# A table of reciprocals stored in another order, its spread as one load a block, and the loads of the output stage in another order on one queue

## The chip, the cores and the metric

The kernel runs on one core of one Trainium2 chip. The metric is the time of one execution in microseconds (us), as a median of several runs. Five engines take part: TensorE (PE; PEld is its weight load), VectorE (DVE), ScalarE (ACT), GpSimd (POOL) and SyncE (SP). SP computes nothing; it issues DMAs, in the order in which they stand in the program, and stops at each until what that DMA needs has happened. ACT and POOL can issue DMAs too, between their other instructions. All queues share 16 DMA engines.

## The reference

Two branches on the same 2048 tokens of width 1024 are mixed by a gate: `out = g * a + (1 - g) * b`. Branch a is attention with 32 heads of width 32, and its output product:

```python
g = sigmoid((x * gate_w).sum(-1, keepdims=True))
qkv = (x @ wqkv).reshape(B, S, 3, H, Dh).transpose(2, 0, 3, 1, 4)
p = softmax(einsum("bhqd,bhkd->bhqk", q, k) * Dh ** -0.5)
o = einsum("bhqk,bhkd->bhqd", p, v)
a = o.transpose(0, 2, 1, 3).reshape(B, S, D) @ wo
```

Branch b looks up one of 64 rows of `u` and `v` for each token and each of 32 router heads (top 1 of 8 times top 1 of 8), and sums `gelu(x . u[e]) * v[e]`. Everything is float32.

## The kernel before, in words

The first 620 us or so make the router, the queries, keys and values; then comes the attention, and from about 1644 us the output product.

**Attention.** Heads are numbered `h = 4 * g + j`, with g the group of four (G = 8) and j in it. A head has NT = 16 steps of 128 keys; `at(step, f)` hangs a piece of work on a step `h * NT + kt`. In a step TensorE makes scores into a ring of 7 PSUM banks (`scores`, L1317), ACT takes their exponential into one of 8 tiles P (L1327), and TensorE multiplies P with V (`pv`, L1338). The sum of P over keys goes three ways: VectorE adds most tiles into `acc` (L1367), POOL adds a few of them into the tile `accd` with accumulating DMAs (L1360, `accd<-P` in the profile), and `merge` (L1370) joins the two. A P tile that such a DMA reads can be written again only when the DMA is done.

**The reciprocals.** `finish` stores a head's unnormalized output to DRAM (`OD`, profile `od<-osb`). `norm_sums` stores its row of sums (`SMD`, profile `smd<-ssb`). For each group of four heads `load_r` loads the sums back as 128 rows of 64 (`rr<-smd`), and `norm_r` takes their reciprocal, multiplies with the gate and stores the result to the table `RD` in DRAM (`rd<-rr`).

**Output.** The 2048 tokens go in 8 blocks of W = 256. For block n, `load_o` loads the heads' outputs of the 8 groups (8 DMAs of 128 KB, `V<-od`), and `load_rb` loads the reciprocals, each row of the table copied to 32 partitions (this is the spread; `rb<-rd` for block 0, `accd<-rd` for the others). `RD` is laid out as group, j, token, so a spread is four DMAs, one for each j, in pieces of 1 KB. The tiles are shared: heads' outputs use the two buffers named V, spreads use the two named accd, so a load waits for the last reader of the block two before. Blocks 0 and 1 use plain products (`wo_mm`): `split_hi`, `split_lo` and `split_o` scale the heads' outputs and cut them into a high and a low part, and `wo_mm` multiplies. Blocks 2 to 7 use a scheme with seven half-size products P1 to P7 (class `Halves`, L963), whose factors on the weight side include T1 to T4; `load_t(i)` brings those from DRAM (tables `t0h`, `t0l` to `t3h`, `t3l`, 1 MB each), the first three into tiles that blocks 0 and 1 have done with. `scale_o(n)` scales a block's heads' outputs on VectorE (L1576), and `unit(n)` makes a block's products and stores its output from the tiles `osb` and `post` (which lies in `rb0`). `plain_out(0)` and `plain_out(1)` store blocks 0 and 1 from `post` as well (L1584, L1586), so the second has to wait until the first's stores have read it.

The last group's reciprocals (kc = KC - 1 = 7) come last, as they need the last head's sums. The order written out by hand in L1597 to L1657 fits blocks 0 and 1, the last reciprocals and the loads of the T factors round that. Work of one engine runs in the order in which it is written.

Of the kernel before, what the change touches and what calls it, by code (L numbers as in the profile page):

```python
# [9 lines left out]
F32 = mybir.dt.float32  # L10
F32R = mybir.dt.float32r
# [5 lines left out]
S = 2048  # L17
D = 1024
H = 32
KC = D // 128  # L20
HC = KC // 2
NT = S // 128
NQ = S // 512
G = H // 4
W = 256
# [6 lines left out]
def gated_mha_peer_kernel(ctx, tc, xT, wqkv, wv, wo, wq, k12, ug, v, out):  # L32
# [8 lines left out]
    nc = tc.nc  # L41
# [4 lines left out]
    dram = ctx.enter_context(tc.tile_pool(name="dram", bufs=1, space=bass.MemoryType.DRAM))  # L46
# [7 lines left out]
    OD = [dram.tile([128, S], F32, name=f"od{g}") for g in range(G)]  # L54
    ZD = dram.tile([1, S], F32, name="zd")
    SMD = [dram.tile([4, S], F32, name=f"smd{g}") for g in range(G)]
    RD = dram.tile([G, 4, S], F32, name="rd")

    TD = [[dram.tile([128, KC // 2, 512], F32R, name=f"t{i}{part}") for part in "hl"] for i in range(4)]
    VPD = [dram.tile([128, D], F32R, name=f"vp{part}") for part in "hl"]  # L60
# [13 lines left out]
    def dma(dst, src, queue=nc.sync):  # L74
        a, b = (ap.bitcast(F32) if ap.dtype == F32R else ap for ap in (dst, src))
        return queue.dma_start(a, b)  # L76
# [16 lines left out]
    def split(hi, lo, src, on=None):  # L93
        nc.scalar.activation(hi, src, AF.Copy)  # L94
        (on or nc.vector).tensor_tensor(out=lo, in0=src, in1=hi.bitcast(F32), op=OP.subtract)
# [13 lines left out]
    def bank():  # L109
        i = bank_no[0] % 8  # L110
        bank_no[0] += 1
        return ps1.tile([128, 512], F32, name=f"bk{i}")
# [788 lines left out]
    zp = Pool("zp", side="right")  # L901
# [357 lines left out]
    wk = Pool("wk", bufs=2)  # L1259
# [88 lines left out]
    def rowsum(ps, *srcs):  # L1348
        for src in srcs:
            for qc in range(NQ):  # L1350
                yield nc.tensor.matmul(ps[32 * qc:32 * qc + 32, :], ones,  # L1351
                                       src[:, qc * 512:(qc + 1) * 512],
                                       start=(src is srcs[0]), stop=(src is srcs[-1]))
# [31 lines left out]
    def norm_sums(h, ps, queue=nc.sync):  # L1385
        g, j = divmod(h, 4)
        o = wk.tile([128, 512], F32, name="ssb")
        ins = nc.scalar.activation(o, ps, AF.Copy)
        dma(SMD[g][j:j + 1, :].rearrange("o (q s) -> (o q) s", q=NQ), o[::32, :], queue)
        return ins  # L1390


    def load_r(g):
        R[g] = wk.tile([128, 128], F32, name="rr", bufs=1)[:, :64]
        dma(R[g], SMD[g].rearrange("j (b m) -> (j b) m", m=64))

    def norm_r(g):
        r = R.pop(g)
        nc.vector.reciprocal(r, r)
        nc.vector.tensor_mul(r, r, G64)  # L1400
        dma(RD[g].rearrange("j (b m) -> (j b) m", m=64), r)


    OC, RB = {}, {}

    def load_o(n, k0, k1, queue=nc.sync):
        if k0 == 0:
            OC[n] = vpool.tile([128, KC, W], F32, name="V")
        for kc in range(k0, k1):
            dma(OC[n][:, kc, :], OD[kc][:, n * W:(n + 1) * W], queue)  # L1410

    def load_rb(n, k0, k1, js=range(4), queue=nc.sync):
        if k0 == 0 and js[0] == 0:
            RB[n] = rb0 if n == 0 else wk.tile([128, KC, W], F32, name="accd")
        for j in js:
            src = RD[k0:k1, j:j + 1, n * W:(n + 1) * W].rearrange("g j s -> j g s")
            dma(RB[n][32 * j:32 * j + 32, k0:k1, :], src.to_broadcast([32, k1 - k0, W]), queue)

    def load_chunk(n, k0, k1, queue=nc.sync):
        load_o(n, k0, k1, queue)  # L1420
        load_rb(n, k0, k1, queue=queue)
# [3 lines left out]
    OH, OL, W0 = {}, {}, []  # L1425
# [19 lines left out]
    def at(step, f, *a):  # L1445
        todo.setdefault(step, []).append((f, a))

    for h in range(H):
        base = h * NT
        g, j = divmod(h, 4)  # L1450
# [18 lines left out]
        at(28 * NT + 6 + i, dma, vhl[:, i], VPD[i])  # L1469
    at(29 * NT + 13, load_o, 0, 0, 4)  # L1470
    at(30 * NT + 7, load_o, 0, 4, KC - 1)
    at(30 * NT + 13, load_rb, 0, 0, KC - 1, range(2))
    at((H - 1) * NT + 2, load_rb, 0, 0, KC - 1, range(2, 4))
    at((H - 1) * NT + 8, load_rb, 1, 0, KC - 1)
    at((H - 1) * NT + 14, load_rb, 2, 0, KC - 1)


    BT = 2
# [34 lines left out]
    def load_at(n):  # L1513
        AT[n] = fin.tile([128, W], F32R, name="at", bufs=3)
        dma(AT[n], ATD[:, n * W:(n + 1) * W])
# [29 lines left out]
    def split_hi(kc):  # L1545
        nc.scalar.activation(woh[kc], raw_wo(kc), AF.Copy)
        if kc < KC - 1:
            o = OC[0][:, kc, :]
            nc.vector.tensor_mul(o, o, RB[0][:, kc, :])
            nc.scalar.activation(OH[0][:, kc, :], o, AF.Copy)  # L1550
# [10 lines left out]
    def load_t(i, *parts):  # L1561

        ops = ht.b.setdefault(f"T{i + 1}", [None, None])
        for n, (part, src) in enumerate(zip(parts, TD[i])):
            if part is None:
                continue
            m = HC // len(part)
            for j, place in enumerate(part):
                dma(place, src[:, m * j:m * j + m, :].rearrange("p k m -> p (k m)"))
            ops[n] = [place[:, k * 512:(k + 1) * 512] for place in part for k in range(m)]  # L1570
# [18 lines left out]
    def split_o(n, k0, k1):  # L1589
        o = OC[n][:, k0:k1, :]  # L1590
        nc.vector.tensor_mul(o, o, RB[n][:, k0:k1, :])
        split(OH[n][:, k0:k1, :], OL[n][:, k0:k1, :], o)

    def banks4():
        return {(i, half): bank() for i in range(W // 128) for half in range(2)}
# [4 lines left out]
    finish(H - 1)  # L1600
    sm = pso.tile([128, 512], F32, name="o")
    list(rowsum(sm, *(P[H - 1, NT - i] for i in (1, 2)), ACC.pop(H - 1)))
    load_o(1, 0, KC - 1, nc.gpsimd)
    split_hi(1)
    for kc in range(1, KC - 1):
        split_hi(kc + 1)
        if kc == 1:
            norm_sums(H - 1, sm, nc.scalar)
            load_r(G - 1)
            for n in range(2):  # L1610
                load_at(n)
            pso.close()
        split_lo(kc)
        wo_mm(pa, 0, [kc], False, False)
    norm_r(G - 1)
    for n in range(2):
        load_chunk(n, KC - 1, KC)
    load_rb(2, KC - 1, KC)
    split_lo(KC - 1)
    split(woh[0], wol[0], raw_wo(0))  # L1620

    load_t(2, None, [fin.tile([128, S], F32R, name="t3l")])
    load_t(0, *([keep.tile([128, S], F32R, name=f"wo_raw{j}")] for j in range(2)))
    ps_odd = Pool("ps_odd", space=PSUM)
    for (i, half), ps in pa.items():
        av_mm(0, i, half, ps)
    split_o(0, KC - 1, KC)
    wo_mm(pa, 0, [KC - 1], False, True)  # L1630
    OH[1] = zp.tile([128, KC, W], F32R, name="z1")
    OL[1] = wk.tile([128, KC, W], F32R, name="acc")
    for k0, k1 in ((0, HC), (HC, KC)):
        split_o(1, k0, k1)
    load_o(2, 0, KC)
    load_at(2)
    load_t(2, [zp.tile([128, S], F32R, name="z0")], None)
    load_t(1, *([keep.tile([128, S], F32R, name=f"wo_raw{2 + j}")] for j in range(2)))
    pa1 = banks4()
    wo_mm(pa1, 1, list(range(KC - 1)), True, False)  # L1640
    for (i, half), ps in pa1.items():
        av_mm(1, i, half, ps)
    plain_out(0, pa)
    load_t(3, *([part[k][:, 512:] for k in range(HC)] for part in (woh, wol)))
    load_rb(3, 0, KC, queue=nc.scalar)
    load_o(3, 0, KC)
    ht.places(wk.tile([128, S], F32R, name="acc"), "A11", "A12")
    ht.places(fin.tile([128, S], F32R, name="s31"), "S3", "S1")
    scale_o(2)
# [121 lines left out]
```

## Time and profile before

| | us |
|---|---|
| median of 3 runs | 1831.14 |
| lowest and highest | 1827.85, 1833.79 |
| the profiled execution, its own time | 1832.25 |
| span of that execution in the trace | 1830.4 |

| engine | busy us | share of the span |
|---|---|---|
| PE | 1817.8 | 99% |
| DVE | 1461.4 | 80% |
| ACT | 1312.5 | 72% |
| POOL | 231.7 | 13% |

The trace names a group of instructions by line, engine, operation and tiles (written from read), with buffer numbers left out. A time in square brackets is how long the engine stood idle before, with what ended that. In the chain of waits each line is a start, a length and what ran; it follows back from the last instruction to what released it. The DMA view can be cut to a stretch of time; for each queue (q1 is SP's, q10 ACT's, q0 POOL's) it then gives packets, MB, and the time of these packets as a share of 16 engines. PEclk and "granted clock" are the share of TensorE's full clock that it was given.

### The profile page before, as it was taken

To read this page: it belongs to the slowest core of one execution; us is meant where nothing else is said; L and a number is where in the kernel's file an instruction comes from. 1 tells how busy PE (TensorE), PEld (TensorE's weight loads), DVE (VectorE), ACT (ScalarE), POOL (GpSimd) and SP (SyncE) were. 2 spreads that over 40 slices of the span, in tenths; PEclk is the share of its full clock that TensorE was granted. 3 is DMA by queue.
4 is the path that set the end of the run, shared out by engine and by line. 5 is a ranking of instruction groups with operands and counts; after the bars stand their busy time and mean duration, and the time that the engine had idled before them with its cause. 6 is when DMAs were issued, how large, how long until landed. Compare 5 with 4: busy or idle time off the path is not lost.

```text
span 1830.4 us, 26559 instructions
## 1 busy us (share of the span) xinstructions
PE 1817.8 (99%) x10083; PEld 1099.8 (60%) x10083; DVE 1461.4 (80%) x1258; ACT 1312.5 (72%) x1716; POOL 231.7 (13%) x358
## 2 busy tenths in 40 slices
PE   9999999999999999999999999999999999999999
PEld 6777777788888644444444444444444444447787
DVE  7866876789967888888888888888888888884675
ACT  5545544522433699999999999999999999992221
POOL 1222222244001100000000000000000000010000
PEclk9999999999999999999999999999999999999999
DMA  7888689660267777776777777777777777776872
GB/s 271 277 277 280 209 296 286 199 215 9 83 240 247 219 157 178 158 177 154 177 176 164 186 165 182 171 173 167 174 186 159 178 159 182 174 138 180 281 164 78
DMA packets 127441, 345.24 MB, mean 189 GB/s; under 512 B 17168, under 2 KB 57904, under 8 KB 107920
## 3 DMA queue, kind: packets, MB, share of 16 engines
q1 hardware_dynamic: 95688, 193.40, 36.0%
q0 software_dynamic: 28224, 145.92, 34.1%
q10 hardware_dynamic: 3400, 4.20, 1.0%
q8 instruction: 80, 1.31, 0.3%
q14 instruction: 49, 0.40, 0.1%
HBM read 171.76 MB, written 72.36 MB: 133 GB/s over the span
## 4 chain that ended last, share of the span: by engine, by line
PE 88%; DMA 5%; issue 3%; DVE 1%; ACT 1%; SPq 1%; POOL 1%; DVEq 0%; ACTq 0%; POOLq 0%
PE ring L1317 28%; PE o L1338 25%; PE bk L302 15%; PE pa L963 5%; PE bk L724 5%; PE bk L982 2%; PE bk L290 2%; PE bk L341 2%; PE ring L1351 1%; PE bk L963 1%; SPq L76 1%; DMA accd<-rd 1%; DMA accd<-P 1%; DMA smd<-ssb 1%; DMA z<-t2h 1%
## 5 line engine op out<-in xcount | busy, mean ns | idle before, releaser
L1327 ACT ACTIVATE P<-ring 128x1024 f32<-128x1024 f32 (+2 forms) x1031 | 912.7, 983 | 14.5 <-DMA accd<-P 1.9
L1367 DVE TENSOR_TENSOR acc<-acc,P 128x2048 f32<-128x2048 f32 x319 | 730.9, 2291 | 72.6 <-ACT P L1327 47.1
L1338 PE MATMUL o<-P,V 128*32 128x512 f32 x3840 | 464.8, 599 | 0.0
L1317 PE MATMUL ring<-Q,K 98*128 98x512 f32 x1024 | 272.2, 407 | 0.4 <-ACT P L1327 0.3
L1317 PE MATMUL ring<-z,z 98*128 98x512 f32 x1020 | 270.6, 407 | 0.6 <-ACT accd L1327 0.6
L1317 PEld LDWEIGHTS ring<-Q,K 98*128 98x128 f32 x1024 | 182.0, 188 | 144.8 <-ACT P L1327 73.8
L1317 PEld LDWEIGHTS ring<-z,z 98*128 98x128 f32 x1020 | 181.3, 188 | 142.8 <-ACT P L1327 72.0
L1338 PEld LDWEIGHTS o<-P,V 128*32 128x32 f32 x3840 | 98.8, 109 | 223.1 <-issue 214.5
L1360 POOL DMA_DIRECT2D accd<-P x95 | 81.5, 858 | 931.5 <-ACT P L1327 406.5
L1365 DVE TENSOR_TENSOR acc<-P,P 128x2048 f32<-128x2048 f32 x32 | 73.4, 2293 | 74.8 <-ACT P L1327 74.8
L302 PE MATMUL bk<-xh,A 128*128 128x512 f32 x336 | 82.8, 396 | 0.0
L302 PE MATMUL bk<-xh,S 128*128 128x512 f32 x336 | 81.3, 393 | 0.0
L302 PE MATMUL bk<-xl,S 128*128 128x512 f32 x336 | 80.1, 391 | 0.0
L135 ACT ACTIVATE hi<-u 128x512 fp32r<-128x512 f32 x42 | 26.5, 632 | 70.0 <-issue 39.4
L302 PEld LDWEIGHTS bk<-xh,A 128*128 128x128 f32 x336 | 62.1, 188 | 23.8 <-issue 5.0
L1370 DVE TENSOR_TENSOR acc<-acc,accd 128x2048 f32<-128x2048 f32 x32 | 73.1, 2284 | 0.0
L302 PEld LDWEIGHTS bk<-xl,S 128*128 128x128 f32 x336 | 62.8, 188 | 16.3 <-issue 2.5
L302 PEld LDWEIGHTS bk<-xh,S 128*128 128x128 f32 x336 | 62.4, 188 | 14.5 <-issue 1.7
L1327 ACT ACTIVATE accd<-ring 128x1024 f32<-128x1024 f32 (+2 forms) x64 | 62.2, 1032 | 2.3 <-PE ring L1317 2.2
L963 PE MATMUL pa<-woh,acc 128*128 128x512 f32 x192 | 62.2, 389 | 0.0
L511 DVE TENSOR_TENSOR u<-u,bk 128x512 f32<-128x512 f32 x70 | 46.6, 682 | 10.0 <-DMA wpd<-u 5.8
L94 ACT ACTIVATE acc<-V 128x512 fp32r<-128x512 f32 x24 | 14.5, 625 | 50.8 <-DVE V L1576 14.4
(302 smaller groups left out, 2204.9 us busy)
## 6 DMA issues: line engine op xcount, KB each, us to landing
accd<-P POOLq DMA_DIRECT2D x95, 1024.0 KB, 7.6
wqt<-in_wq SPq DMA_DIRECT2D x64, 512.0 KB
wraw<-in_wqkv SPq DMA_DIRECT2D x28, 512.0 KB
kdh<-hi POOLq DMA_DIRECT2D x32, 256.0 KB, 5.3
kdl<-lo POOLq DMA_DIRECT2D x32, 256.0 KB, 6.5
qdh<-hi POOLq DMA_DIRECT2D x32, 256.0 KB, 5.9
qdl<-lo POOLq DMA_DIRECT2D x32, 256.0 KB, 5.9
z<-kdh SPq DMA_DIRECT2D x32, 256.0 KB
```

The costliest lines, as they stand in the source:

```text
L290: nc.tensor.matmul(b0[w, n], AW[PLAIN[w, ki]][a][:, k, :], X[f"B{ki + 1}{n + 1}"][b][:, k, :], start=first, stop=last)
L302: nc.tensor.matmul(ps, a[i][:, k, :], b[j][:, k, :], start=(k == 0 and i == j == 0), stop=(k == HC - 1 and i == 1))
L511: nc.vector.tensor_tensor(out=out, in0=a, in1=b, op=OP.add)
L724: nc.tensor.matmul(ps, x_part(a, t // 4, kc)[:, tok], b, start=first, stop=last)
L963: nc.tensor.matmul(ps, self.a[a][i][:, k, :], self.b[b][j][k], start=(not first and k == 0 and i == j == 0), stop=(k == HC - 1 and i == 1))
L1317: on_ring(nc.tensor.matmul(ring[:, i, :], K[:98, kt * 128:(kt + 1) * 128], Q[:98, qc * 512:(qc + 1) * 512], start=True, stop=True), i)
L1327: on_ring(nc.scalar.activation(P[h, kt][:, q0 * 512:(q0 + m) * 512].rearrange("p (a m) -> p a m", a=m), ring[:, i:i + m, :], AF.Exp, scale ...
L1338: nc.tensor.matmul(O[h][32 * qc:32 * qc + 32, :], Vt[g][:, kt, 32 * j:32 * j + 32], p[:, qc * 512:(qc + 1) * 512], start=(kt == 0), stop=( ...
L1360: nc.gpsimd.dma_start(ACCD[h], P[h, kt], accum_op=OP.add)
L1365: nc.vector.tensor_add(ACC[h], P[h, 0], P[h, kt])
L1367: nc.vector.tensor_add(ACC[h], ACC[h], P[h, kt])
L1370: nc.vector.tensor_add(ACC[h], ACC[h], ACCD[h])
```

## The change

1. `RD` is laid out as j, block, group, token within the block, so that a block's reciprocals of one j are 8 KB in one piece. `norm_r` stores into it with the indices to match.
2. `load_rb` is one DMA: 4 rows of up to 8 KB, each copied to 32 partitions. Before it was four DMAs.
3. In the attention loop block 0's spread was issued in two halves (head 30, step 13, and head 31, step 2); it is issued whole at the first place. Block 2's first seven groups were spread at head 31, step 14; that goes, and the whole spread of block 2 is loaded in the output stage.
4. Block 1's heads' outputs were loaded through POOL's queue right after the last head; they are loaded on SP behind the last sums. Block 3's spread was issued by ACT behind block 1's products; SP issues it, and block 3's heads' outputs, ahead of them.
5. `norm_r(G - 1)` stands inside the loop over kc, at kc = 4, instead of behind it. The first half of block 1 is scaled and split ahead of block 0's last group. Block 2's heads' outputs are loaded ahead of T1 instead of behind it.

```diff
-    RD = dram.tile([G, 4, S], F32, name="rd")
+    RD = dram.tile([4, S // W, KC, W], F32, name="rd")
...
-        dma(RD[g].rearrange("j (b m) -> (j b) m", m=64), r)
+        dma(RD[:, :, g, :].rearrange("j n (q m) -> (j n) q m", m=64), r)
...
-    def load_rb(n, k0, k1, js=range(4), queue=nc.sync):
-        if k0 == 0 and js[0] == 0:
+    def load_rb(n, k0, k1, queue=nc.sync):
+        if k0 == 0:
             RB[n] = rb0 if n == 0 else wk.tile([128, KC, W], F32, name="accd")
-        for j in js:
-            src = RD[k0:k1, j:j + 1, n * W:(n + 1) * W].rearrange("g j s -> j g s")
-            dma(RB[n][32 * j:32 * j + 32, k0:k1, :], src.to_broadcast([32, k1 - k0, W]), queue)
+        src = RD[:, n, k0:k1, :].rearrange("j g s -> j (g s)")[:, None]
+        dma(RB[n][:, k0:k1, :].rearrange("p g s -> p (g s)"),
+            src.to_broadcast([4, 32, (k1 - k0) * W]), queue)
...
-    at(30 * NT + 13, load_rb, 0, 0, KC - 1, range(2))
-    at((H - 1) * NT + 2, load_rb, 0, 0, KC - 1, range(2, 4))
+    at(30 * NT + 13, load_rb, 0, 0, KC - 1)
     at((H - 1) * NT + 8, load_rb, 1, 0, KC - 1)
-    at((H - 1) * NT + 14, load_rb, 2, 0, KC - 1)
...
-    load_o(1, 0, KC - 1, nc.gpsimd)
     split_hi(1)
     for kc in range(1, KC - 1):
...
             for n in range(2):
                 load_at(n)
+            load_o(1, 0, KC - 1)
             pso.close()
         split_lo(kc)
         wo_mm(pa, 0, [kc], False, False)
-    norm_r(G - 1)
+        if kc == HC:
+            norm_r(G - 1)
     for n in range(2):
         load_chunk(n, KC - 1, KC)
-    load_rb(2, KC - 1, KC)
+    load_rb(2, 0, KC)
     split_lo(KC - 1)
     split(woh[0], wol[0], raw_wo(0))
...
     load_t(2, None, [fin.tile([128, S], F32R, name="t3l")])
+    OH[1] = zp.tile([128, KC, W], F32R, name="z1")
+    OL[1] = wk.tile([128, KC, W], F32R, name="acc")
+    split_o(1, 0, HC)
+    split_o(0, KC - 1, KC)
+    load_o(2, 0, KC)
     load_t(0, *([keep.tile([128, S], F32R, name=f"wo_raw{j}")] for j in range(2)))
...
-    split_o(0, KC - 1, KC)
     wo_mm(pa, 0, [KC - 1], False, True)
-    OH[1] = zp.tile([128, KC, W], F32R, name="z1")
-    OL[1] = wk.tile([128, KC, W], F32R, name="acc")
-    for k0, k1 in ((0, HC), (HC, KC)):
-        split_o(1, k0, k1)
-    load_o(2, 0, KC)
+    split_o(1, HC, KC)
     load_at(2)
...
+    load_rb(3, 0, KC)
+    load_o(3, 0, KC)
     pa1 = banks4()
     wo_mm(pa1, 1, list(range(KC - 1)), True, False)
...
-    load_rb(3, 0, KC, queue=nc.scalar)
-    load_o(3, 0, KC)
```

## The prediction, made before the changed kernel was run

> **What bounds the kernel now.** I read the page first, then TensorE's waits, the chain of waits in order of time, the timelines round each gap, and the DMA view cut to short windows. The page says that TensorE is the bound:
>
> ```profile
> span 1830.4 us, 26559 instructions
> PE 1817.8 (99%) x10083; PEld 1099.8 (60%) x10083; DVE 1461.4 (80%) x1258; ACT 1312.5 (72%) x1716; POOL 231.7 (13%) x358
> ```
>
> So only about 12.6 us of the span are not matmul time, and part of that is the start and the end. The waits of TensorE from 1600 us on (waiting line, releaser, total, times, longest) are all that an edit of the last stages can win back directly:
>
> ```profile
> PE pa L963 <- DVE rb L969: 2.3, 1, 2.3
> PE pa L1522 <- ACT z L94: 1.4, 1, 1.4
> PE pa L963 <- ACT osb L1678: 0.8, 1, 0.8
> PE ring L1317 <- ACT P L1327: 0.3, 1, 0.3
> ```
>
> That is 4.5 us in the output stage and 0.3 us in the attention loop. The largest costs more than itself. In windows (stretch, length, busy time of PE, PEld, DVE, ACT, POOL, granted clock, DMA share, GB/s) the clock stays at 1.00 round the 1.4 us gap, and falls right after the 2.3 us one:
>
> ```profile
> 1660.00:1680.00 20.00, 18.61 (x82) 15.06 (x81) 9.82 (x12) 3.51 (x5) 0.00 (x0) 1.00 0.60 195
> 1722.00:1724.00 2.00, 1.27 (x3) 1.08 (x4) 1.97 (x4) 0.00 (x0) 0.00 (x0) 0.71 0.66 82
> 1724.00:1726.00 2.00, 2.00 (x6) 1.57 (x5) 1.22 (x3) 1.15 (x2) 0.00 (x0) 0.50 0.71 81
> 1726.00:1728.00 2.00, 2.00 (x9) 1.60 (x9) 2.00 (x4) 0.00 (x0) 0.00 (x0) 0.94 0.65 86
> ```
>
> 2 x (0.29 + 0.50 + 0.06) = 1.7 us are lost to the low clock. In all 4.5 + 1.7 = 6.2 us, 0.34%, is the most that the output stage can give.
>
> **What releases those gaps.** The chain (start, length, what):
>
> ```profile
> 1599.79 10.48 DMA accd<-P
> 1650.21 10.26 DMA smd<-ssb
> 1660.54 2.29 DMA rr<-smd
> 1663.70 1.46 DMA rd<-rr
> 1689.23 9.99 DMA z<-t2h
> 1740.03 13.60 PE pa L963 x60
> 1760.88 13.60 PE pa L963 x60
> ```
>
> The 1.4 us gap ends the serial path of the last head's sums: store, load, reciprocal, store to RD, spread, scale. Its first step is an 8 KB store that takes 10.26 us, because it stands behind other transfers. The last two rows are the same place in two later blocks, 20.85 us apart: a block's time without gaps. The 0.8 us gap waits for t2h. The 2.3 us gap waits for VectorE, which came late to a product's sums because block 3's heads (V<-od) came late.
>
> **The change, part by part.** *How wide the new spread is.* I read the number of engines off the small store of the sums, which has four rows. In the window 1632 to 1664 us it is all that the ScalarE queue carries (queue, packets, MB, share):
>
> ```profile
> q10 hardware_dynamic: 8, 0.01, 0.1%
> ```
>
> Eight packets are four rows and four completions, so four engines. The store od<-osb, whose DRAM side also begins with a dimension of 4, runs out between 1659.9 and 1661.4 us nearly alone:
>
> ```profile
> q1 hardware_dynamic: 23, 0.05, 7.7%
> ```
>
> 7.7% of 16 engines is 1.2 engines. The new load begins with 4 on the DRAM side (j, then 32 copies, then up to 8 KB), so I take four engines, with 32 pieces each; the old ones begin with 32. The other end, 16 engines, is a rival below. A piece of 8 KB, seen from 1676 to 1677.5 us where only such pieces run:
>
> ```profile
> q1 hardware_dynamic: 77, 0.63, 99.7%
> ```
>
> 1.5 x 16 x 0.997 / 77 = 0.311 us. A full block's spread is then 32 x 0.311 = 10.0 us on four engines, and one of 7 KB pieces 8.7 us. The old spread, in 1 KB pieces, from 1740 to 1746 us:
>
> ```profile
> q1 hardware_dynamic: 500, 0.48, 67.3%
> ```
>
> 0.48 MB in 6 us is 80 GB/s, 13 us for 1.05 MB, on all engines. So the load itself gets little shorter; twelve engines come free, and four carry all of it.
>
> *Block 0's spread, now in one piece (a loss).* Before, half of it went out at step 13 of head 30 and half at head 31. The issue on SP, ScalarE, the accumulating DMA behind it on POOL, and the waits:
>
> ```profile
> 1598.41 1.03 SPq L76 DMA_DIRECT2D rb<-rd  x2
> 1597.73 11.69 ACT L1327 ACTIVATE P<-ring 128x512 f32<-128x512 f32 x13
> 1599.79 0.86 POOL L1360 DMA_DIRECT2D accd<-P  x1 [13.26 <-ACT P L1327]
> 1610.35 3.77 ACT L1327 ACTIVATE P<-ring 128x512 f32<-128x512 f32 x4 [0.93 <-DMA accd<-P]
> 1611.00 0.50 PE L1317 MATMUL ring<-Q,K 98*128 98x512 f32 x1 [0.31 <-ACT P L1327]
> ```
>
> ScalarE already waits 0.93 us for this accumulation to release a P tile, and TensorE 0.31 us. Between 1599.6 and 1603 us the queues carry the first row, between 1605.2 and 1607.2 us the second:
>
> ```profile
> q1 hardware_dynamic: 313, 0.31, 54.3%
> q0 software_dynamic: 52, 0.43, 102.2%
> ```
>
> No accumulation packet (q0) ran while the spread (q1) did: on an engine the later transfer stands behind the earlier. Its eight pieces an engine take 8 x (2 x 16 x 1.022 / 52 = 0.63) = 5.0 us. The new spread holds four engines from about 1599.3 for 8.7 us, to 1608.0; the accumulation there ends at 1613.0 and lands at about 1613.3, not 1610.27. ScalarE then waits 3.05 us longer, and TensorE's eighth score matmul with it, as its ring bank is freed only then. ScalarE, which worked 11.69 us without a break ahead of that wait, can't win it back. The gap becomes 3.4 us, over the 2.3 us that dropped the clock, so up to 1.7 us more; as part of the slow window falls in the gap itself I take 1.3. Loss: 4.35 us. Bounds: 0 if the pieces interleave, 6.9 at the old 80 GB/s (0.92 MB in 11.5 us; 5.9 + 1.0).
>
> *Block 1's and 2's spreads, and the sums.* The rows that follow are VectorE in the loop over kc, TensorE at kc = 5 and at the gap, and a ScalarE pass:
>
> ```profile
> 1655.50 0.42 DVE L1556 TENSOR_TENSOR acc<-V,z 128x256 fp32r<-128x256 f32 x1
> 1656.17 1.22 DVE L1553 TENSOR_TENSOR wol<-wo_raw,woh 128x1024 fp32r<-128x1024 f32 x1
> 1661.38 1.07 PE L1522 MATMUL pa<-wol,z 128*128 128x512 f32 x4
> 1669.27 1.20 PE L1522 MATMUL pa<-woh,z 128*128 128x512 f32 x4 [1.39 <-ACT z L94]
> 1670.85 1.06 ACT L94 ACTIVATE z<-V 128x1024 fp32r<-128x1024 f32 x1 [1.63 <-DVE V L1591]
> ```
>
> Block 1's spread (head 31, step 8) has no accumulation behind it; issued near 1632, behind one accumulation, it ends by about 1646. Block 2's leaves the loop, and V<-od for block 1 leaves POOL's queue, so nothing stands ahead of the store of the sums at 1650.21. Like rd<-rr it then takes about 1.5 to 2.2 us, not 10.26. rr lands at about 1654.8. The reciprocal, now in the loop at kc = 4, comes to VectorE's turn at 1655.9: no wait. Its 0.8 us hides in the 4 us by which the splits lead TensorE (1657.4 against 1661.4); behind it are queued the splits of kc = 5 and 6, and were rr still as late as 1662.8, about 3 us of matmuls would wait for them. SP issues seven loads of block 1's heads (7 x 0.5, as in the row of 1598.41) ahead of rd<-rr, so that goes out at 1657.2 and is there at 1658.7; the spread of row 7 lands at about 1662. VectorE, 0.8 us later than before, does half of block 1 first (1.22, ScalarE 1.06, 1.22) and reaches block 0's last scale at 1666.1; its high half stands at 1667.1, ahead of the 1669.27 - 1.39 = 1667.9 at which TensorE needs it. Gain 1.4 us, with 0.8 to spare; each us that the sums come later than that brings back one of it.
>
> *The T loads and blocks 2 and 3.* SP issues block 2's spread at about 1660.7, four issues later, T3's low half, block 2's heads, T1, T3's high half, T2, block 3's spread, block 3's heads, then block 0's outputs. The program lets eight DMAs of SP and ScalarE be in flight, so an issue waits for the landing of the eighth before it; the old order paid for that here:
>
> ```profile
> 1672.59 15.92 SPq L76 DMA_DIRECT2D V<-od  x8
> SPq L76 <- DMA accd<-rd: 11.8, 4, 8.3
> ```
>
> In the new order the four engines carry the sum. With 2.5 us for each MB of T (421 GB/s, the 1676 window) and 2.7 for heads or outputs (1.54 MB in 4 us from 1708 on):
>
> ```profile
> q1 hardware_dynamic: 1069, 1.54, 103.6%
> ```
>
> Block 2's spread begins at 1663.4, after the two small ones. + 10.0 + 2.5 + 2.7 + 5.0 + 0.3 + 2.5 + 5.0 + 10.0 + 2.7 = 1704.1. T3 high lands by 1687, so the 0.8 us gap goes. Outputs of block 0 can't be issued before block 3's spread has landed (the eighth issue back from block 3's last head load), so the first lands at about 1705.8, where the old one let VectorE copy at 1704.88:
>
> ```profile
> 1704.88 0.69 DVE L1586 COPY rb<-pa 128x512 f32<-128x512 f32 x1 [3.16 <-PE pa L963]
> 1713.45 1.23 DVE L1576 TENSOR_TENSOR V<-V,accd 128x1024 f32<-128x1024 f32 x1 [3.99 <-DMA V<-od]
> 1721.90 1.41 DVE L969 TENSOR_TENSOR rb<-rb,pa 128x512 f32<-128x512 f32 x2
> 1722.73 0.67 PE L963 MATMUL pa<-z,s 128*128 128x512 f32 x1 [2.26 <-DVE rb L969]
> ```
>
> From the first copy to the sum that frees TensorE's bank it took 1722.6 - 1704.88 = 17.7 us, of which 3.99 + 0.61 were waits for V<-od. Without them 13.1 us: 1718.9, say 1719.2 as the outputs land one after another. So this matmul starts at 1719.2, not 1722.73: 3.5 us, in which the two small gaps are contained. TensorE would be ready at 1722.73 - 2.26 - 1.4 - 0.8 = 1718.3, so about 0.9 us of gaps stay, shorter than the 1.4 us one that left the clock alone: another 1.7 us. Gain 5.2 us. T4 lands by 1712 to 1713, about when its product starts. Later blocks ask 10.0 + 2.7 + 2.7 us of those four engines in 20.85 us, so the steady blocks stay covered.
>
> *Sum.* -5.2 + 4.35 = -0.85 us on the profiled 1832.25 (span 1830.4), which stands 1.1 us above the median. On the median, 1831.14 - 0.85 = **1830.3**.
>
> **The rivals.** *Interleaving (faster).* If an engine alternated between SP's and POOL's queues, the accumulation would need 8 x (0.63 + 0.27) = 7.2 us from about 1601.5 and land at 1609, before ScalarE asks. Then only the 5.2 us and the old 0.3 count: 1825.6. Against it stands the window without a q0 packet. [...]
>
> *All 16 engines (faster).* The new load doesn't narrow: 0.92 MB at 421 GB/s is 2.2 us, the accumulation isn't held, no gap of the output stage is left: 6.2 + 0.3, 1824.6. Against it: the od<-osb row. [...]
>
> *Reading one row 32 times stays slow (slower).* The four engines together get no more than the old 80 GB/s, 13 us a block. Block 0's spread then costs 6.9 us in the loop. Spreads 2 and 3 add 3 us each ahead of the outputs, so the bank comes free at 1725.2, 2.5 us later than before, and the low clock stays. Sum 9.4: 1840.5. It decides from about 11.7 us a block on: 3.4 us more ahead of the outputs eat the 3.5 gained there and keep the clock low, and the loop loses 4.35 + 1.5. For it: the only spreads seen run at this rate. Against it: they read one 1 KB row from 16 engines at once; now four engines read four rows.
>
> **How the numbers follow.** Chances: forecast 0.38, interleaving 0.13, 16 engines 0.14, slow rows 0.35. About 0.3%, 5.5 us, is what a measurement of this kernel can tell from no change. The forecast's own range is -4.5 to +4 (the clock kept or lost at either place, a spread 5% off), 1826.6 to 1835.1; three tenths of its chance lie past the bound, half on each side (0.06 and 0.06). The fast rivals lie at the bound or just past it: 0.23 of their 0.27 count as faster. Of the slow rows' 0.35, 0.31 count as slower. Faster 0.06 + 0.23 = 0.29; slower 0.06 + 0.31 = 0.37; the same 0.34. Range: from the fast rivals to the slow one, 1824 to 1841.
>
> **What would show it.** Right: a spread's packets number a quarter of the engines' share for 9 to 10 us; accd<-P near 1600 takes 13 to 14 us; ScalarE waits about 4 us there and TensorE over 3; smd<-ssb under 3 us; no wait of line 1522; the gap before the third block's second product under 2 us with the clock at 1.00. Wrong: accd<-P at 10 us or less, smd<-ssb still near 10, a spread over 12 us, or a wait for T or V that isn't named here.

## The result, and the profile after

The changed kernel takes 1853.31 us (median; 1851.34 to 1860.2) against 1830.97 us (1827.85 to 1833.97): ratio 1.0126, 95% interval 1.0106 to 1.0145. That is 22.3 us slower, and outside the predicted range of 1824 to 1841. The profiled execution took 1855.12 us.

The page of the changed kernel:

```profile
span 1853.3 us, 26507 instructions
PE 1820.4 (98%) x10083; PEld 1099.7 (59%) x10083; DVE 1461.5 (79%) x1258; ACT 1312.8 (71%) x1716; POOL 227.6 (12%) x351
```

The span grew by 22.9 us, TensorE's busy time only by 2.6. The other 20 us are idle time of TensorE. Its waits from 1590 us on, in the columns of the prediction:

```profile
PE pa L1527 <- DVE rb L1584: 15.5, 1, 15.5
PE ring L1317 <- ACT P L1327: 4.9, 1, 4.9
PE pa L963 <- DVE rb L969: 3.0, 1, 3.0
PE pa L963 <- DMA z<-t2h: 1.4, 1, 1.4
PE pa L963 <- DVE acc L95: 0.3, 1, 0.3
```

They sum to 25.1 us where before had 4.8. The old 1.4 us wait on the last sums is gone; the one in the attention grew from 0.3 to 4.9; and a new one of 15.5 us stands at the product (L1527) that needs a PSUM bank which `plain_out(1)` (VectorE's copy, L1584) has yet to empty. Windows round the two large ones (stretch, length, busy PE, PEld, DVE, ACT, POOL, granted clock, DMA share, GB/s):

```profile
1608.00:1614.00 6.00, 3.71 (x24) 1.62 (x23) 5.79 (x3) 2.43 (x3) 0.00 (x0) 0.94 0.25 71
1614.00:1620.00 6.00, 3.36 (x17) 0.89 (x17) 0.34 (x2) 3.77 (x4) 0.86 (x1) 0.50 0.57 137
1684.00:1690.00 6.00, 6.00 (x28) 4.99 (x27) 0.00 (x0) 0.00 (x0) 0.00 (x0) 1.00 0.25 87
1714.00:1722.00 8.00, 0.00 (x0) 0.00 (x0) 0.00 (x0) 0.00 (x0) 0.00 (x0) 0.82 0.25 79
1728.00:1732.00 4.00, 2.72 (x6) 2.15 (x7) 1.98 (x3) 1.51 (x3) 0.00 (x0) 0.50 0.92 300
```

Two things are to be seen. The clock is at half behind both gaps, which accounts for most of TensorE's 2.6 extra busy us. And the DMA share is 0.25 in the third and the fourth row: four engines of sixteen, for many us on end, at 79 to 87 GB/s, while every computing engine but TensorE is idle in the third and all of them in the fourth. The DMA view of the third stretch (queue, packets, MB, share of 16 engines):

```profile
q1 hardware_dynamic: 67, 0.52, 25.0%
```

6 x 4 / 67 = 0.36 us for a piece of 8 KB. SyncE's issues show who waits for the four engines (SPq rows are issues, x their number; the second of the two `accd<-rd` at 1668.32 is block 2's spread, issued at 1669.05):

```profile
1658.99 0.32 SPq L76 DMA_DIRECT2D rr<-smd  x1
...
1668.32 1.25 SPq L76 DMA_DIRECT2D accd<-rd  x2
1669.66 0.42 SPq L76 DMA_DIRECT2D t3l<-t2l  x1
1673.93 19.58 SPq L76 DMA_DIRECT2D V<-od  x8
1693.55 0.43 SPq L76 DMA_DIRECT2D wo_raw<-t0h  x1
...
1696.70 0.53 SPq L76 DMA_DIRECT2D accd<-rd  x1
1697.33 28.21 SPq L76 DMA_DIRECT2D V<-od  x8
1725.65 2.07 SPq L76 DMA_DIRECT2D out<-rb  x4
```

In these rows an issue waits for the landing of the eighth before it. So the seventh of block 2's heads waited until block 2's spread had landed, at 1690.9, and the eighth until T3's low half had, at 1693.2; T1's halves, T3's high half and all behind them went out from 1693.55 on. Block 3's heads were held in the same way by block 3's spread, and block 0's outputs, which stand behind them, went out at 1725.65. SP's own waits between 1660 and 1760 us say it in one row:

```profile
SPq L76 <- DMA accd<-rd: 28.8, 2, 14.6
```

These are two waits of about 14.5 us for a spread. In the attention, ScalarE waits for the accumulation, which now shares engines with block 0's spread:

```profile
1615.99 3.77 ACT L1327 ACTIVATE P<-ring 128x512 f32<-128x512 f32 x4 [5.56 <-DMA accd<-P]
```

### The profile page after: what moved, and what is told of

It is laid out like the page before. It is cut to its first block, busy times and chain, and to the rows that moved or that the text cites. A ratio compares the mean times of both kernels' runs of the same rounds, so it can differ in the third digit from the quotient of the medians.

```text
span 1853.3 us, 26507 instructions
## 1 busy us (share of the span) xinstructions
PE 1820.4 (98%) x10083; PEld 1099.7 (59%) x10083; DVE 1461.5 (79%) x1258; ACT 1312.8 (71%) x1716; POOL 227.6 (12%) x351
## 4 chain that ended last, share of the span: by engine, by line
PE 86%; DMA 8%; issue 3%; DVE 2%; ACT 1%; POOL 1%; SPq 1%; ACTq 0%; DVEq 0%; POOLq 0%
PE ring L1317 27%; PE o L1338 25%; PE bk L302 15%; PE bk L724 5%; PE pa L963 4%; DMA accd<-rd 3%; PE bk L982 2%; PE bk L290 2%; PE bk L341 2%; DMA accd<-P 2%; PE ring L1351 1%; DMA t3l<-t2l 1%; PE bk L963 1%; SPq L76 1%; DMA xl<-in_wo 0%
## 5 line engine op out<-in xcount | busy, mean ns | idle before, releaser
L1317 PE MATMUL ring<-Q,K 98*128 98x512 f32 x1024 | 272.2, 407 | 5.0 <-ACT P L1327 4.9
L1317 PE MATMUL ring<-z,z 98*128 98x512 f32 x1020 | 270.7, 407 | 0.8 <-ACT accd L1327 0.6
L1317 PEld LDWEIGHTS ring<-Q,K 98*128 98x128 f32 x1024 | 182.2, 188 | 149.3 <-ACT P L1327 78.4
L1317 PEld LDWEIGHTS ring<-z,z 98*128 98x128 f32 x1020 | 181.3, 188 | 143.1 <-ACT P L1327 72.3
L302 PEld LDWEIGHTS bk<-xh,S 128*128 128x128 f32 x336 | 62.4, 188 | 14.5 <-issue 1.7
```

Of the source, the lines that this page charges most:

```text
L302: nc.tensor.matmul(ps, a[i][:, k, :], b[j][:, k, :], start=(k == 0 and i == j == 0), stop=(k == HC - 1 and i == 1))
L1317: on_ring(nc.tensor.matmul(ring[:, i, :], K[:98, kt * 128:(kt + 1) * 128], Q[:98, qc * 512:(qc + 1) * 512], start=True, stop=True), i)
```

## The experiments

Three theories stood at the start. A: the one load is narrow, and four engines are what it costs. B: reading the same row of the table over and over is slow on any number of engines. C: the order on SP costs the time whatever form the spread has. In the table a ratio compares a kernel with runs of the kernel before from the same batch; those had medians from 1829.79 to 1831.93 us, so medians of different rows can't be told apart to less than 2 us.

| kernel | median us | ratio to before | 95% interval |
|---|---|---|---|
| changed kernel | 1853.31 | 1.0126 | 1.0106 to 1.0145 |
| new order, four loads of 8 KB pieces | 1824.92 | 0.9967 | 0.9957 to 0.9977 |
| old order, one load | 1855.62 | 1.0134 | 1.0112 to 1.0156 |
| new order, old layout, four loads of 1 KB pieces | 1845.15 | 1.0074 | 1.0055 to 1.0092 |
| old order, four loads of 8 KB pieces | 1825.78 | 0.9976 | 0.9967 to 0.9985 |
| changed, block 0's spread in two parts | 1860.62 | 1.0166 | 1.0145 to 1.0187 |
| changed, block 0's spread as four loads | 1850.62 | 1.0107 | 1.0090 to 1.0123 |
| changed, block 3's loads behind block 0's outputs | 1854.63 | 1.0136 | 1.0119 to 1.0152 |
| four loads, block 0's in the attention as one | 1832.65 | 1.0000 | 0.9991 to 1.0010 |
| four loads, blocks 2 and 3 as one | 1843.75 | 1.0065 | 1.0046 to 1.0084 |
| four loads, blocks 4 to 7 as one | 1829.47 | 0.9991 | 0.9979 to 1.0003 |

**Four loads of 8 KB pieces, new order.**

```diff
-        src = RD[:, n, k0:k1, :].rearrange("j g s -> j (g s)")[:, None]
-        dma(RB[n][:, k0:k1, :].rearrange("p g s -> p (g s)"),
-            src.to_broadcast([4, 32, (k1 - k0) * W]), queue)
+        for j in range(4):
+            src = RD[j:j + 1, n, k0:k1, :].rearrange("j g s -> j (g s)")
+            dma(RB[n][32 * j:32 * j + 32, k0:k1, :].rearrange("p g s -> p (g s)"),
+                src.to_broadcast([32, (k1 - k0) * W]), queue)
```

> The changed kernel, but a spread is four loads, one for each j, of 32 pieces of 8 KB (the table's new layout stays, the order stays). Theory A, the width: in the changed kernel a piece of 8 KB takes about 0.4 us of one engine, and 32 such pieces in a row on each of only four engines make the 13 to 15 us of a block; a load that starts with 32 runs on 16 engines, so a spread takes 3 to 4 us, accd<-P near 1600 about 11 us, the waits of 4.9 and 15.5 us go: about 1826 us. Theory B, the row: reading one row of the table again and again gives some 80 GB/s whoever reads it (1 KB pieces on all engines before, 8 KB pieces on four engines after); the spread then still takes 11 to 13 us, now on all engines, and the time stays at 1848 to 1858 us. Theory C, the order on SP: the outputs of block 0 still stand behind three spreads and the T loads; with short spreads that is about 6 us less than before, so about 1840 us.

Measured: 1824.92 us, ratio 0.9967. It is faster than before, as theory A said; B and C asked for 1840 or more. The page of this kernel:

```profile
span 1823.5 us, 26540 instructions
PE 1816.1 (100%) x10083; PEld 1098.1 (60%) x10083; DVE 1461.5 (80%) x1258; ACT 1312.4 (72%) x1716; POOL 227.5 (12%) x351
```

No wait of TensorE is left from 1590 us on, and the clock stays at 1.00; the window in which the changed kernel has its longest gap:

```profile
1690.00:1720.00 30.00, 30.00 (x134) 24.86 (x133) 14.48 (x22) 6.42 (x11) 0.00 (x0) 1.00 0.96 276
```

**The one load alone.** The old order and queues of the output stage; layout, `norm_r` and `load_rb` of the changed kernel. The expectation speaks of block 0's spread cut at group 4; the kernel that ran issues it whole at head 30, step 13, as the changed kernel does:

```diff
-    at(30 * NT + 13, load_rb, 0, 0, KC - 1, range(2))
-    at((H - 1) * NT + 2, load_rb, 0, 0, KC - 1, range(2, 4))
+    at(30 * NT + 13, load_rb, 0, 0, KC - 1)
```

> The kernel before with the new layout and the one-load spread alone; its order and queues stay. Block 0's spread is cut into groups 0 to 3 and 4 to 6, at the two steps where its halves stood. Theory A: every spread takes 13 to 15 us on four engines as in the changed kernel; block 2's seven groups issued at the end of head 31 hold the small store of the sums on those engines, so the sums come some us later than before, and block 3's spread lands late too: 1834 to 1842 us. Theory B: a spread costs what it did, 13 us: 1830 to 1834 us. Theory C, nearly all in the order: 1831 us, the same as before.

Measured: 1855.62 us. All theories had it too low, A by 14 us (and A for a spread of block 0 in two parts). The one load does the whole damage without the new order of the output stage; only the places differ:

```profile
PE ring L1317 <- ACT P L1327: 5.2, 1, 5.2
PE pa L1521 <- ACT z L94: 5.2, 1, 5.2
PE pa L963 <- ACT acc L94: 3.7, 1, 3.7
PE pa L963 <- DVE rb L969: 2.3, 2, 2.1
```

They sum to less than in the changed kernel, but TensorE is busy for 1826.8 us, 9.0 more than before, at a mean granted clock of 0.993 against 0.999.

**The order alone.** The changed kernel with the old `RD`, the old store and the old four loads in `load_rb`:

```diff
-        src = RD[:, n, k0:k1, :].rearrange("j g s -> j (g s)")[:, None]
...
+        for j in range(4):
+            src = RD[k0:k1, j:j + 1, n * W:(n + 1) * W].rearrange("g j s -> j g s")
+            dma(RB[n][32 * j:32 * j + 32, k0:k1, :], src.to_broadcast([32, k1 - k0, W]), queue)
```

> The changed kernel with the table's old layout and the old spread, four loads in pieces of 1 KB; the new order and the whole spread of block 0 at head 30, step 13, stay. Theory A: the old spread is on all engines and lets others in between its four parts; the wait for block 0's outputs falls from 15.5 to about 6 us, the head's wait stays near 5: about 1842 us. Theory B and theory C alike: a spread still takes 13 us, all engines are held meanwhile, and the outputs of block 0 stand behind two of them: 1848 to 1856 us. It parts A from the others: under 1845 for A, over 1848 for C.

Measured: 1845.15 us, between the two bounds. Two waits are left, the same two places as in the changed kernel:

```profile
PE pa L1527 <- DVE rb L1584: 9.7, 1, 9.7
PE ring L1317 <- ACT P L1327: 5.4, 1, 5.4
```

So the new order by itself, block 0's whole spread in the attention included, costs some 14 us with the old spread in 1 KB pieces. Theory C holds under a condition: the order is only as good as its spreads are short.

**Four loads of 8 KB pieces, old order.** The edit of the first experiment, made to the kernel before with the new layout; block 0's halves by j as before.

```diff
-    RD = dram.tile([G, 4, S], F32, name="rd")
+    RD = dram.tile([4, S // W, KC, W], F32, name="rd")
...
-            src = RD[k0:k1, j:j + 1, n * W:(n + 1) * W].rearrange("g j s -> j g s")
-            dma(RB[n][32 * j:32 * j + 32, k0:k1, :], src.to_broadcast([32, k1 - k0, W]), queue)
+            src = RD[j:j + 1, n, k0:k1, :].rearrange("j g s -> j (g s)")
+            dma(RB[n][32 * j:32 * j + 32, k0:k1, :].rearrange("p g s -> p (g s)"),
+                src.to_broadcast([32, (k1 - k0) * W]), queue)
```

> The kernel before with the new layout and a spread as four loads of 8 KB pieces (7 KB for seven groups), one for each j, that start with 32; its order, its queues and the two halves of block 0's spread stay as they were. With the new order the same four loads gave 1824.9 us. Theory A, the width and the pieces do it all: spreads of 6 us let the sums, t2h and block 3's heads arrive in time in the old order too: 1824 to 1826 us, no gap over 0.3 us. Theory C, the order does part of it: the small store of the sums still stands behind block 1's heads on GpSimd's queue and block 2's spread, and block 3's heads still come late: gaps of 1.4 and about 1 us stay, 1827 to 1831 us.

Measured: 1825.78 us, as theory A said; no wait of TensorE from 1590 us on. With four loads of 8 KB pieces the order makes no difference that can be told (0.9976 and 0.9967, intervals overlapping). With the two runs before this one the table has both orders for each of three forms of the spread: 1830.97 and 1845.15 (1 KB pieces), 1855.62 and 1853.31 (one load), 1825.78 and 1824.92 (four loads of 8 KB pieces). Block 0's spread goes out whole in the new order and in two halves in the old, but for the one load, where it is whole in both.

**The spreads by themselves.** Behind the last output of the kernel with four loads, twice:

```diff
+    X = wk.tile([128, KC, W], F32, name="accd")
+    for n in range(2):
+        for j in range(4):
+            src = RD[j, :, n, :]
+            dma(X[32 * j:32 * j + 32], src[None].to_broadcast([32, KC, W]))
+        src = RD[:, n].rearrange("j g s -> j (g s)")[:, None]
+        dma(X.rearrange("p g s -> p (g s)"), src.to_broadcast([4, 32, KC * W]))
+        for j in range(4):
+            src = RD[j:j + 1, n].rearrange("j g s -> j (g s)")
+            dma(X[32 * j:32 * j + 32].rearrange("p g s -> p (g s)"), src.to_broadcast([32, KC * W]))
+        for rows in (16, 128):
+            src = TD[n][0].rearrange("p k m -> p (k m)")[:rows][:, None]
+            dma(X.rearrange("p g s -> p (g s)"), src.to_broadcast([rows, 128 // rows, KC * W]))
```

> The changed kernel with four-load spreads, and behind its last output, twice over, loads of 1 MB each into one tile, so that one starts when the one before has landed: four loads of 1 KB pieces (eight rows of 1 KB for each j, each read 32 times), the one load of 4 rows of 8 KB, the four loads of one row of 8 KB each, one load of 16 rows of 8 KB with 8 copies of each, and one of 128 rows, each read once. They measure the spread with nothing beside it. Theory A, the width: 13 us, 32 x 0.31 = 10 us, 3 to 4 us, 3 us, 2.5 us. Theory B, the row: time goes with how often a row is read and how many engines read it at once: 13 us, 12 to 14 us, 6 us as seen inside the kernel, 2.5 to 4 us for 16 rows, 2.5 us. It tells whether the 13 to 15 us of a block in the changed kernel are its own or come from what runs beside it. The added loads lengthen the kernel by about their sum, some 70 us.

The run took 1922.48 us. Measured, in windows cut to the packets of each load (the first round's 1 KB form overlapped the last outputs and is left out): first round one load, four loads, 16 rows, 128 rows; second round 1 KB pieces and the same four.

```profile
1838.50:1850.90 12.40, 0.00 (x0) 0.00 (x0) 0.00 (x0) 0.00 (x0) 0.00 (x0) 0.50 0.23 85
1852.30:1857.30 5.00, 0.00 (x0) 0.00 (x0) 0.00 (x0) 0.00 (x0) 0.00 (x0) 0.50 0.91 210
1859.40:1864.40 5.00, 0.00 (x0) 0.00 (x0) 0.00 (x0) 0.00 (x0) 0.00 (x0) 0.50 0.92 210
1866.00:1869.60 3.60, 0.00 (x0) 0.00 (x0) 0.00 (x0) 0.00 (x0) 0.00 (x0) 0.50 0.80 291
1870.80:1883.50 12.70, 0.00 (x0) 0.00 (x0) 0.00 (x0) 0.00 (x0) 0.00 (x0) 0.50 0.44 83
1885.20:1900.60 15.40, 0.00 (x0) 0.00 (x0) 0.00 (x0) 0.00 (x0) 0.00 (x0) 0.50 0.23 68
1902.00:1907.30 5.30, 0.00 (x0) 0.00 (x0) 0.00 (x0) 0.00 (x0) 0.00 (x0) 0.50 0.91 198
1909.40:1914.10 4.70, 0.00 (x0) 0.00 (x0) 0.00 (x0) 0.00 (x0) 0.00 (x0) 0.50 0.91 223
1915.70:1919.20 3.50, 0.00 (x0) 0.00 (x0) 0.00 (x0) 0.00 (x0) 0.00 (x0) 0.50 0.85 300
```

With nothing beside it the one load takes 12.4 and 15.4 us at a share of 0.23, as long as the old form in 1 KB pieces (12.7). Four loads take 5.0 and 5.3. Both theories have a part: the width is worth a factor of 2.5 to 3, and reading rows again one of 1.3 to 1.5 (16 rows and four loads against 128 rows). The 10 us that A and the prediction expected were measured in neither round, and why the second took 3 us longer than the first isn't known.

**Which spreads cost.** The kernel with four loads, with the one load for some blocks only; the condition is `n == 0 and k0 == 0`, `n in (2, 3)` or `n >= 4`.

```diff
+        if n in (2, 3):
+            src = RD[:, n, k0:k1, :].rearrange("j g s -> j (g s)")[:, None]
+            dma(RB[n][:, k0:k1, :].rearrange("p g s -> p (g s)"),
+                src.to_broadcast([4, 32, (k1 - k0) * W]), queue)
+            return
```

> The changed kernel with four-load spreads everywhere (1824.9 us, no gap) except block 0's in the attention, which is the one load. It prices the stall in the attention against a clean output stage. From the changed kernel's trace: accd<-P 15 us, ScalarE's wait 5 to 6 us, TensorE's 4.4 to 5.2 us, and half a clock for 6.8 us, of which some 1.5 us are lost outside the gap. If nothing of it is given back: 1830 to 1832 us. Rival: the output stage has slack to give back, 1825 to 1828 us.

> The same with the one load for blocks 2 and 3 alone, four loads for all others. It prices the two spreads ahead of block 0's outputs. If they make the wait of 15.5 us: block 0's outputs go out 15 to 20 us later than in the kernel with four loads everywhere (1699.2), TensorE waits 10 to 16 us there, and the time is 1838 to 1845 us. Rival, that the spreads of blocks 4 to 7 keep the bound (each holds four engines for 12 to 15 us of a block's 20.85 us, beside heads and outputs): under 1835 us.

> The same with the one load for blocks 4 to 7 alone, four loads for all others. By themselves such loads took 12.25 and 15.25 us against 20.85 us for a block, so they should stay covered: 1825 to 1826 us, no wait. Rival: with the heads and the outputs on the same four engines they don't fit, and a wait of VectorE for the spread shows at each block, of some 2 us each: 1829 to 1834 us.

Measured: 1832.65, 1843.75 and 1829.47 us. By the ratios, against 0.9967 for four loads everywhere: 0.0033 x 1831 = 6.0 us for block 0, 17.9 for blocks 2 and 3, 4.4 for blocks 4 to 7. They sum to 28.3; the one load everywhere costs (1.0126 - 0.9967) x 1831 = 29.1. By the intervals each price is good to 2.5 to 4 us. Each has its own wait of TensorE. Block 0 as one load:

```profile
PE ring L1317 <- ACT P L1327: 5.0, 1, 5.0
```

Blocks 2 and 3 as one load (L1590 is the copy in `plain_out` again, six lines further down in this kernel):

```profile
PE pa L1533 <- DVE rb L1590: 14.8, 1, 14.8
```

Blocks 4 to 7 as one load:

```profile
PE pa L963 <- DVE rb L969: 3.3, 1, 3.3
```

The first run came out just above what was expected, 1832: nothing of the attention's stall is given back. The second came out as expected (block 0's outputs go out at 1718.25, 19 us later than with four loads everywhere): the two spreads ahead of block 0's outputs make the wait of 15.5 us. In the third I had expected no wait. Block 4's spread, issued behind the T4 loads, block 1's outputs and its own heads, lands 19.19 us later, and VectorE waits for it; a row of the chain and one of VectorE's timeline:

```profile
1713.82 19.19 DMA accd<-rd
```

```profile
1733.04 2.36 DVE L1580 TENSOR_TENSOR V<-V,accd 128x1024 f32<-128x1024 f32 x2 [10.26 <-DMA accd<-rd]
```

The rival had the right time, but not for its reason, a wait at each block: VectorE waits 10.26 us for block 4's spread and under 2 us for two later ones, and TensorE has one wait that counts, in block 3, while VectorE is late with scaling block 4.

**Block 3's loads later.**

```diff
-    load_rb(3, 0, KC)
-    load_o(3, 0, KC)
     pa1 = banks4()
...
     plain_out(0, pa)
+    load_rb(3, 0, KC)
+    load_o(3, 0, KC)
```

> The changed kernel with block 3's spread and heads' outputs issued by SP right behind block 0's outputs instead of ahead of block 1's products. The reading is that SP could issue block 0's outputs only at 1725.65 because block 3's spread had to land first, and that plain_out(1) and with it TensorE waited 15.5 us for them. If so, the outputs go out near 1704, the wait of 15.5 us falls under 3 us; block 3's heads come some 5 us later and the wait behind them (3.0 us) grows to 5 to 8 us: 1840 to 1847 us. Rival: the T loads set it, which are late in either order, and the heads of block 3 give it all back: 1850 us or more.

Measured: 1854.63 us, the rival's time. Block 0's outputs go out at 1697.43, and the wait of 15.5 us is gone, but others take its place. The two largest, and a row of the chain:

```profile
PE pa L963 <- ACT acc L94: 9.2, 1, 9.2
PE pa L963 <- DMA wol<-t3l: 3.9, 1, 3.9
```

```profile
1703.40 25.74 DMA accd<-rd
```

What holds block 3's heads is again block 3's spread, which lands 25.74 us after its issue, where by itself it took 12.4 and 15.4. SP issues it behind the T loads (from 1694.29 on) and block 0's outputs. So the T loads, the rival's cause, look to be a part of it. Four engines have the same work whatever the order; the order chooses who waits for them.

**Block 0's spread in two parts.**

```diff
-    at(30 * NT + 13, load_rb, 0, 0, KC - 1)
+    at(30 * NT + 13, load_rb, 0, 0, 4)
+    at((H - 1) * NT + 2, load_rb, 0, 4, KC - 1)
```

> The changed kernel, but block 0's spread goes out in two parts, groups 0 to 3 at head 30, step 13, and groups 4 to 6 at head 31, step 2 (the two places of before), each still on four engines. The reading of the two traces is that the whole spread holds the accumulation accd<-P (15.1 us) and costs 4.6 us of TensorE's wait and about 1.7 us of clock there. If that holds: accd<-P near 11 us, TensorE's wait under 1 us, and the time falls by 5 to 6.5 us, to about 1847 us, as all that follows comes that much earlier. Rival: the later part goes out near the load of block 1's spread and moves the stall on, or the last chain of loads doesn't start earlier: under 2 us of gain.

Measured: 1860.62 us, a miss of 13 us. The wait at L1317 fell only from 4.9 to 3.4 (accd<-P from 15.1 to 13.25): even four groups of seven keep the four engines busy beside the accumulation (issued at 1601.24; from 1608 to 1614 us the two queues take 19.0% and 4.7% of 16 engines, 3.8 engines). Waits sum to 22.7, less than in the changed kernel, but TensorE is busy for 1826.0 us, 5.6 more, as the clock is at half in three stretches of the output stage, where the changed kernel has one; one of them:

```profile
1723.00:1737.00 14.00, 4.91 (x12) 3.85 (x13) 3.89 (x6) 2.35 (x4) 0.00 (x0) 0.51 0.65 210
```

Why the output stage then waits where it does isn't settled by this run.

**Block 0's spread as four loads.** The changed kernel, with the four loads for `n == 0 and k0 == 0` alone.

> The changed kernel with block 0's spread alone as four loads (16 engines), all other spreads as one load. It prices the stall in the attention by itself: accd<-P near 1600 at 10 to 11 us, TensorE's wait there under 0.5 us and no drop of the clock. Theory A: the rest follows 6 us earlier, 1846 to 1848 us. Rival, after the run in which block 0's spread went out in two parts: what the attention wins, the output stage gives back in waits: 1851 to 1856 us.

Measured: 1850.62 us. The stall in the attention is gone, and SP's issue of block 0's outputs comes 7.6 us earlier (1718.02). The time falls by about 3 us, with overlapping intervals, not by the 6 that the same edit is worth in the other direction when the output stage is clean: the waits of 15.6 and 3.3 stay, and the mean granted clock is 0.994, as in the changed kernel, although that one has 6.83 us at half clock from the attention's stall.

## Why the prediction was wrong

*What held.* The bound: 6.2 us in the output stage and 0.3 in the attention were called the most that could be won there, and the kernel with four loads has no gap left at 1824.9 us, against the 1824.6 worked out for a load on all 16 engines. The width: four engines, from the store with four rows, is a share of 0.25 in the rows above. The stall in the attention: block 0's spread does hold up the accumulation, and ScalarE and TensorE wait for it; the size was 4.9 us of TensorE's wait, not 3.4, and 6.0 us of the time in the run that prices it alone, not 4.35. The sums' path: the load of the sums went out at 1658.99, 1.8 us after the issue of their store, where it was over 10 us before, and no wait for them is left.

*The step that failed first* is the price of a spread: "a full block's spread is then 32 x 0.311 = 10.0 us on four engines". The 0.311 came from T loads, in which 16 engines read each row once. By itself the one load took 12.4 and 15.4 us, with a piece at 0.36 and 0.44 us in the mean. In place it is worse, as a piece took longer while other loads ran on the other twelve engines: the 24 pieces of 8 KB that began between 1677 and 1681 us, beside block 2's heads, took 0.65 us on average, those between 1686 and 1690, with nothing beside them, 0.36. Why they take longer is open. Rows of the chain of the changed kernel:

```profile
1600.79 15.12 DMA accd<-P
...
1669.66 23.51 DMA t3l<-t2l
...
1696.70 28.50 DMA accd<-rd
```

Block 2's spread and T3's low half together were put at 12.5 us. The half, issued right behind the spread, landed 23.51 us after its issue, as its pieces on the four engines came behind the spread's. Block 3's spread, behind T1 to T3, landed 28.50 us after its issue.

*The second step* is the sum along the four engines, 40.7 us from the first piece of block 2's spread at 1663.4 to the last of block 3's heads at 1704.1, behind which block 0's outputs come. In the packets of the trace it goes from 1670.7 to 1727.4, 56.7 us. Of the 16.0 us more, 15.2 are the price of the two spreads: block 2's took some 20.0 us (1670.7 to 1690.7) and block 3's 15.2 (about 1710 to 1725.2), where 10.0 each were put in. The other terms held together. The start came 7.3 us late; 6.6 of it is the attention's stall carried on (the load of the sums went out at 1652.40 in the kernel with four loads, which has no stall), and TensorE is as late. So a forecast gain of 5.2 us in the output stage became a loss of some 16: 17.9 for blocks 2 and 3 and 4.4 for the later ones, against a kernel without gaps that stands 6 us below before.

*The third* is "on an engine the later transfer stands behind the earlier". The DMA view from 1602.5 to 1606.5 us and, below it, from 1608 to 1614 us (q0 is the accumulation, q1 the spread):

```profile
q0 software_dynamic: 73, 0.60, 72.9%
q1 hardware_dynamic: 35, 0.25, 26.1%
```

```profile
q0 software_dynamic: 26, 0.20, 15.7%
q1 hardware_dynamic: 32, 0.23, 9.5%
```

In the first stretch the spread has its four engines to itself (0.261 x 16 = 4.2) and the accumulation the other twelve. In the second the two shares sum to four engines: both run on the same four, by turns. In the packets of the trace a turn is a single piece, 0.63 us for the accumulation and 0.29 for the spread. So the accumulation was behind the spread for some 6 us and then shared with it, and landed at 1615.9 (the chain's first row above), not at 1613.3. It is the interleaving of the rival from about 1607.7 us on, with its 7.2 us for eight pieces nearly right (they ended at 1615.3), but not its start, which had the accumulation land at 1609. Ahead of the first turn the four engines took 52 pieces of the spread, 13 each, from 1600.8 us on. The turns begin as the other twelve engines finish their part of the accumulation, near 1607.5 us; what holds it back on the four until then stays open.

*The rivals.* "Reading one row 32 times stays slow" had the right sign. Its 13 us a block is about what the load takes by itself, and its 6.9 us for block 0 came near the 6.0 measured. Its sum, 9.4 us, was too small by more than half, because it added 3 us for each of two spreads, which took 10.0 and 5.2 us more than forecast, and nothing for the later blocks. "Later blocks stay covered" failed by 4.4 us. The forecast did see that four engines carry all of a spread, and added up their work; the price of a piece that it put into the sum was that of another kind of load, with nothing beside it.

## What to carry to other kernels

Ask of each load on how many DMA engines it runs, and price every later load by its share on the fullest of them: here T3's low half landed only when those four were through, 23.51 us after its issue. Take the price of a piece from a load that reads in the same way, beside the same traffic: 0.31 us for 8 KB became 0.36 to 0.65. A broadcast that starts with few rows can be narrow: here one load with 4 rows first took 12 to 15 us for 1 MB at a share of 0.23, and four loads that start with 32 copies took 5 at 0.91, with the same long pieces. With the four loads the order no longer mattered, and TensorE had no gap in either order.

## What the runs showed of the hardware

Pieces of 1 KB from a row read 32 times by themselves ran at 83 GB/s with the 16 engines busy for only 0.44 of the time, and no run shows what paced them; in pieces of 8 KB from one row, 16 engines got 198 to 210 GB/s, and from 128 rows read once 291 to 300. And the length of a gap alone doesn't decide the clock: behind a gap of 3.3 us in block 3 it stayed at 1.00 (with blocks 4 to 7 as one load), where it fell behind one of 2.3 us in the kernel before:

```profile
1738.00:1742.00 4.00, 0.71 (x4) 0.31 (x3) 3.15 (x6) 0.63 (x1) 0.00 (x0) 1.00 0.36 99
1742.00:1748.00 6.00, 6.00 (x27) 4.94 (x28) 4.78 (x8) 1.48 (x3) 0.00 (x0) 1.00 0.38 127
```

Where a gap falls may matter. In the traces of the kernel before and of the changed one each stretch at half clock inside the kernel lasts a multiple of 3.41 us (3.41 in the kernel before, 6.83 and 13.65 in the changed one), and the two of the changed kernel begin 105.81 us apart, 31 times 3.41. Cut into steps of 3.41 us from the start of such a stretch, between 1590 and 1815 us, both traces together have two steps at full clock in which TensorE was idle for over 1.94 us (2.26 in the kernel before, 3.41 in the changed one), and both were followed by half clock; none with under 1.57 was; in between, the one with 1.57 was, and those with 1.82 and 1.94 were not. The 2.3 us gap of the kernel before lies whole in one step. The gap of 3.0 us in the changed kernel, which ends at 1768.69, is parted between two, 1.2 and 1.8, and the clock stayed at 1.00. How the one of 3.3 us lies in such steps is not shown.
